# Gram products of a gated delta rule kernel: two runs of one array tile shape each, in place of two shapes in turn

## The chip, the cores and the metric

The kernel runs on one core of a Trainium2 chip. The metric is the device time of one execution in microseconds (us). Before the change three runs gave 435.13, 436.81 and 437.67 us, so the median is 436.81 us. Of one further execution there is a profile, with a trace of every instruction.

## The reference

For 4 x 8 pairs of batch and head there is a state of 48 x 48 numbers. Over 768 steps it is read and corrected, and what it gives goes through two weight matrices with a softplus between them:

```python
k_n = k / (norm(k) + 1e-6)
for t in range(768):
    y[t]  = g[t] * (q[t] @ state)
    state = state + beta[t] * outer(k_n[t], v[t] - state.T @ k_n[t])
x   = y, transposed and reshaped to (3072, 384)
out = softplus(x @ w_in) @ w_out          # w_in 384 x 2048, w_out 2048 x 384
```

## The kernel before

The 768 steps are cut into six rounds of 128 (`cc` in the code), and a round into two chunks of 64 steps (`cl`). Inside a chunk the recurrence is solved in closed form, so that it becomes small matrix products; from chunk to chunk only the state is handed on. The 32 pairs of batch and head are held as p (two groups), i (four pairs of heads), m (which head of the pair) and r (which half of the batches).

A round runs through these stages, and the names are those of the rows further down:

- k, q, v and g are loaded by SP (L299), four transfers for each tensor and round. k is squared on ACT (`ksq`, L380), summed on DVE (L387), brought to a norm (on POOL, L424, from the second round on), and scaled to `kn` (L446); q is cast to `qn` (L467).
- TensorE transposes `kn` and `qn` (L489) and ACT copies the result to `kqt` (L512): features on the partitions, 64 columns of queries and then 64 of keys. Feature rows of m = 0 lie on partitions 0 to 47, those of m = 1 on 64 to 111.
- The Gram products follow (function `gram`), four times in a round, 24 times in all: for each i, r and m a product of the 64 keys with all 128 columns (L531), and a product of the last 32 keys with the 64 keys (L535), which puts two blocks of the key products a second time into other partitions. That is 32 matmuls, each with a weight load of its own. L531 uses a 64 x 64 tile of the array (48 rows by 64 columns are filled), L535 a 64 x 32 tile (48 by 32 filled). Here they are called a gram.
- ACT copies the key products, negated, to `kk` (L553), DVE masks the query products to `mt` (L572). Both read the PSUM buffers that the gram wrote; five buffers of this kind (`p_d`) serve all small products.
- When the four grams of a round are read out, DVE transposes `kk` to `ln` (L595), and a triangular solve of 15 steps follows, on DVE in the first round and on POOL in the others (L617, then L628 and L635). DVE and ACT bring its result back (`tn` L661 and L671, `t` L683 and L691), and small matmuls finish the inverse (L710, L745, L755, L796, L799).
- The state chain goes chunk by chunk through L843, L886, L899, L925, L954, L981, L997 and L1020; the output of a chunk comes from L843 and L1038, is multiplied with g (L1071) and transposed (L1088, L1098).
- The two large products, with w_in (L1122, softplus on ACT in L1143) and w_out (L1160, copied out in L1182 and stored in L1191), fill the rest of TensorE's time. L1122 has 512 moving columns in the four middle rounds, 256 in the first and the last; L1160 has 384.

The order in which each engine gets its instructions is fixed when the program is built. `Plan.run` goes through items with an engine, a cost, dependencies and a priority, and always places the item that can start first. The gram is one item of cost 0.4 and 32 matmuls; what stands inside the item is the planner's only as a number of matmuls. Grams have the priority of an early stage of their round, so those of a round stand among the large products of the rounds before it. Engines take their instructions in order, so an instruction that waits holds up all behind it on its engine.

Of the kernel before, what the change touches and what calls it, by code (L numbers as in the profile page):

```python
# [41 lines left out]
class Plan:  # L42
# [6 lines left out]
    def add(self, eng, cost, fn, deps=(), bufs=(), prio=0, tail=0.1, order=(), mm=0, dma=0):  # L49
        it = Item()  # L50
        it.eng, it.cost, it.fn = eng, cost, fn
        it.deps = [d for d in deps if d is not None]
        it.bufs, it.prio, it.tail, it.end = list(bufs), prio, tail, None
        it.n = len(self.items)
        it.order = [d for d in order if d is not None]
        it.mm, it.dma = mm, dma
        for b in it.bufs:
            b.users += 1
        self.items.append(it)
        return it  # L60
# [94 lines left out]
def kernel(  # L155
# [11 lines left out]
    nc = tc.nc  # L167
    B, H, S, D = q.shape
    P = 128
    C = 64  # L170
    HC = 32
    NSS = S // 128
    NP = H // 2
# [101 lines left out]
    def f16ps(ap):  # L275
        return ap.bitcast(F16)

    HALF = [slice(0, 64), slice(64, 128)]
    FEAT = [slice(0, D), slice(64, 64 + D)]
    QUAD = [slice(32 * i, 32 * i + 32) for i in range(4)]  # L280
# [81 lines left out]
    for cc in range(NSS):  # L362
# [117 lines left out]
        for cl in cls:  # L480
            for p in range(2):
                tp, kq = Buf(p_d), Buf(r_kqt)
                kqt[cl, p] = kq

                def trs(a=kn[cl], b=qn[cl], p=p, tp=tp):
                    o = f16ps(tp.ap).rearrange("p (i r j t) -> p i r j t", r=2, j=2, t=C)
                    for j, x in ((1, a), (0, b)):
                        for i in range(NP):
                            nc.tensor.transpose(  # L489
                                o[:, i, :, j],  # L490
                                x.ap[:, p, 2 * i : 2 * i + 2].rearrange(
                                    "p h d -> p (h d)"
                                ),
                                ident,
                            )

                t1 = add(
                    "PE",
                    0.5,
                    trs,  # L500
                    deps=[kn_it[cl], qn_it[cl]],
                    bufs=[kn[cl], qn[cl], tp, kq],
                    prio=pl + 6,
                    tail=0.2,
                    mm=8,
                )

                kqt_it[cl, p] = [
                    add(
                        "ACT",  # L510
                        1.02,
                        lambda tp=tp, kq=kq: nc.scalar.copy(  # L512
                            kq.ap.rearrange("p n c -> p (n c)"), f16ps(tp.ap)
                        ),
                        deps=[t1],
                        bufs=[tp, kq],
                        prio=pl + 6,
                    )
                ]
                gp = [Buf(p_d), Buf(p_d)]  # L520
                mt[cl, p] = [Buf(r_mt), Buf(r_mt)]

                def gram(kq=kq, gp=gp):


                    for i in range(NP):
                        for r in range(2):
                            for m in range(2):
                                x = kq.ap[FEAT[m], 2 * i + r]
                                o = gp[m].ap.rearrange("p (i c) -> p i c", i=NP)  # L530
                                nc.tensor.matmul(o[HALF[r], i], x[:, C:], x)  # L531
                                o = gp[m].ap.rearrange(
                                    "p (i x c) -> p i x c", i=NP, c=HC
                                )
                                nc.tensor.matmul(  # L535
                                    o[QUAD[2 * r + 1], i, 0:3:2], x[:, C + HC :], x[:, C:]
                                )

                t2 = add(
                    "PE",  # L540
                    0.4,
                    gram,
                    deps=kqt_it[cl, p],
                    bufs=gp + [kq, kk] + mt[cl, p],
                    prio=pl + 6,
                    tail=0.2,
                    mm=32,
                )
                mt_it[cl, p] = []
                for m in range(2):  # L550

                    def kkc(g=gp[m], kk=kk, u0=16 * cl + 8 * p + m):
                        nc.scalar.activation(  # L553
                            kk.ap[:, :, u0 : u0 + 7 : 2].rearrange("p x i t -> p i x t"),
                            g.ap.rearrange("p (i x t) -> p i x t", i=NP, x=4)[:, :, 0:3:2],
                            AF.Copy,
                            scale=-1.0,
                        )

                    kk_it[cl].append(  # L560
                        add(
                            "ACT",
                            0.4,
                            kkc,
                            deps=[t2],
                            bufs=[gp[m], kk],
                            prio=pl + 6,
                        )
                    )

                    def mask_m(g=gp[m], o=mt[cl, p][m]):
                        nc.vector.tensor_tensor(  # L572
                            o.ap,
                            g.ap.rearrange("p (i t) -> p i t", i=NP)[:, :, :C],
                            mask[:, None, :].broadcast_to([P, NP, C]),
                            ALU.mult,
                        )

                    mt_it[cl, p].append(
                        add(  # L580
                            "DVE",
                            0.42,
                            mask_m,
                            deps=[t2],
                            bufs=[gp[m], mt[cl, p][m]],
                            prio=pl + 8,
                        )
                    )
# [114 lines left out]
        for cl in cls:  # L703
            us = range(16 * cl, 16 * cl + 16)
# [20 lines left out]
        for gr in groups:  # L725
            us = slice(16 * gr[0], 16 * gr[-1] + 16)
# [47 lines left out]
        for gr in groups:  # L774
            us = slice(16 * gr[0], 16 * gr[-1] + 16)
# [334 lines left out]
        for job in jobs:  # L1110
# [40 lines left out]
            for gi in [2 * cl + p for cl in job for p in range(2)]:  # L1151
                cl, p = gi // 2, gi % 2
# [73 lines left out]
```

## Time and profile before

| what | value |
|---|---|
| median of three runs | 436.81 us |
| profiled execution | 435.81 us, span of the core's instructions 433.9 us |
| TensorE matmuls busy | 382.2 us (88% of the span), 6384 matmuls |
| DVE, ACT, POOL busy | 139.2, 159.4, 108.5 us |
| mean granted TensorE clock | 0.756 of full speed |
| matmuls of the gram | L531 109.5 us and L535 84.5 us busy, 384 each; their spans overlap one another |
| large products | L1122 85.5 us, L1160 80.5 us busy, 384 each |

A row of the timeline gives start, length, engine, line, operation and shapes, and in brackets how long the engine was idle before it and what ended that. A matmul's end is modelled, so lengths of neighbours overlap: what a matmul costs in a stream is the distance from its start to the next one's start. The granted clock stands as a share of full speed, where 1.00 is 2.4 GHz and 0.50 is 1.2 GHz.

### The profile page before, as it was taken

Reading aid. Unit: us, or ns where it says so; the run is one execution under the profiler, and the core shown is the slowest. Engines: PE = TensorE matmul, PEld = TensorE weight load, DVE = VectorE, ACT = ScalarE, POOL = GpSimd, SP = SyncE. Lnnn points to the kernel's source line nnn. Section 1 sums busy time; section 2 is a strip of 40 time slices with the busy share of each in tenths; the row PEclk is TensorE's granted clock in tenths of the full one; section 3 lists DMA queues with packets and bytes.
Section 4 is the critical chain, followed back from the end, with each engine's and each line's share of the span. In section 5 each row is a group of like instructions: output and inputs, shape, how many; then the busy total and the mean of one; then the engine's idle time right before and its main releaser. Section 6 shows DMA issues by size and latency. Waiting matters only on the chain.

```text
span 433.9 us, 13899 instructions
## 1 busy us (share of the span) xinstructions
PE 382.2 (88%) x6384; PEld 235.1 (54%) x6384; DVE 139.2 (32%) x278; ACT 159.4 (37%) x272; POOL 108.5 (25%) x202
## 2 busy tenths in 40 slices
PE   0699599468899999999999589999999999999895
PEld 0555355355676655455466466546555555656572
DVE  2421950535523131420426133264311054232101
ACT  3331221536572320233354324345141553564250
POOL 7210600385040000740097002228200055000000
PEclk9955555558888855668699555679867979999999
DMA  9999993008910963200011916007100000200202
GB/s 128 170 156 194 174 185 56 2 5 132 156 22 11 149 108 39 54 2 0 2 39 41 147 34 117 2 2 112 38 19 23 3 2 22 57 5 20 56 18 56
DMA packets 106458, 27.73 MB, mean 64 GB/s; under 512 B 100768, under 2 KB 106016, under 8 KB 106400
## 3 DMA queue, kind: packets, MB, share of 16 engines
q1 hardware_dynamic: 103680, 23.60, 35.9%
q0 software_dynamic: 2720, 3.24, 4.4%
q8 instruction: 50, 0.82, 0.9%
q14 instruction: 8, 0.07, 0.1%
HBM read 25.26 MB, written 4.72 MB: 69 GB/s over the span
## 4 chain that ended last, share of the span: by engine, by line
PE 81%; issue 7%; ACT 4%; DVE 3%; SPq 2%; DMA 1%; POOL 1%; ACTq 0%; POOLq 0%; DVEq 0%
PE h L1122 18%; PE d L531 17%; PE o L1160 16%; PE d L535 12%; PE d L489 3%; SPq L299 2%; PE d L843 2%; PE d L1038 2%; PE d L899 2%; PE d L954 2%; PE d L755 1%; PE d L1088 1%; PE d L997 1%; PE d L799 1%; DMA kf<-in_k_dram 1%
## 5 line engine op out<-in xcount | busy, mean ns | idle before, releaser
L531 PE MATMUL d<-kqt 48*64 48x128 f16 x384 | 109.5, 285 | 1.5 <-ACT kqt L512 1.3
L1122 PE MATMUL h<-xt,w_in 128*128 128x512 f16 (+1 forms) x384 | 85.5, 369 | 0.0
L535 PE MATMUL d<-kqt 48*32 48x64 f16 x384 | 84.5, 220 | 0.0
L1160 PE MATMUL o<-w_out,ga 128*128 128x384 f16 x384 | 80.5, 355 | 2.8 <-DVE osb L1182 2.6
L1143 ACT ACTIVATE ga<-h 128x512 f16<-128x512 f32 x96 | 57.1, 598 | 59.4 <-PE h L1122 57.5
L553 ACT ACTIVATE kk<-d 128x256 f16<-128x256 f32 x48 | 18.1, 383 | 126.3 <-PE d L535 100.7
L572 DVE TENSOR_TENSOR mt<-d,mask 128x256 f16<-128x256 f32 x48 | 19.3, 422 | 122.7 <-ACT kk L553 93.1
L531 PEld LDWEIGHTS <-kqt 48*64 48x64 f16 x384 | 44.6, 116 | 25.8 <-issue 2.2
L535 PEld LDWEIGHTS <-kqt 48*32 48x32 f16 x384 | 36.0, 94 | 38.6 <-issue 0.3
L1160 PEld LDWEIGHTS <-ga 128*128 128x128 f16 x384 | 38.6, 105 | 30.8 <-issue 11.3
L1122 PEld LDWEIGHTS <-w_in 128*128 128x128 f16 x384 | 37.6, 106 | 26.1 <-issue 10.9
L424 POOL TENSOR_TENSOR ss<-ss,half_c 128x32 f32<-128x32 f32 (+1 forms) x6 | 27.8, 4631 | 86.1 <-DVE ss L387 86.1
L1182 DVE COPY osb<-o 128x384 f32<-128x384 f32 x24 | 13.3, 555 | 62.1 <-PE o L1160 62.1
L617 POOL TENSOR_TENSOR nn<-ln,beta_l 128x256 f32<-128x256 f16 x10 | 6.0, 617 | 104.6 <-DVE ln L595 104.6
L1071 DVE TENSOR_TENSOR yg<-d,gf 128x384 f16<-128x384 f32 x24 | 13.2, 553 | 54.5 <-PE d L1038 54.3
L635 POOL TENSOR_TENSOR tt<-tt,tmp 128x30 f32<-128x30 f32 (+7 forms) x75 | 28.9, 386 | 5.9
L628 POOL TENSOR_TENSOR tmp<-nn,tt 128x30 f32<-128x30 f32 (+7 forms) x75 | 27.9, 372 | 5.9
L512 ACT COPY kqt<-d 128x1024 f16<-128x1024 f16 x24 | 23.7, 1011 | 14.9 <-PE d L489 14.9
L489 PE MATMUL d<-ident,kn 128*128 128x128 f16 x96 | 13.2, 282 | 12.5 <-DVE kn L446 12.2
L489 PE MATMUL d<-ident,qn 128*128 128x128 f16 x96 | 13.2, 281 | 5.9 <-POOL qn L467 4.6
L925 ACT CAST u<-d 128x384 f16<-128x384 f32 x24 | 11.1, 485 | 16.1 <-PE d L899 16.1
L489 PEld LDWEIGHTS <-kn 128*128 128x128 f16 x96 | 8.9, 129 | 14.8 <-DVE kn L446 12.2
(71 smaller groups left out, 340.1 us busy)
## 6 DMA issues: line engine op xcount, KB each, us to landing
kf<-in_k_dram SPq DMA_DIRECT2D x24, 192.0 KB, 5.5
qf<-in_q_dram SPq DMA_DIRECT2D x24, 192.0 KB, 5.6
vf<-in_v_dram SPq DMA_DIRECT2D x24, 192.0 KB, 4.4
gf<-in_g_dram SPq DMA_DIRECT2D x24, 192.0 KB, 5.4
out_dram<-osb SPq DMA_DIRECT2D x48, 96.0 KB, 2.2
w_in<-in_moe_w_in_dram POOLq DMA_DIRECT2D x1, 1536.0 KB, 11.4
w_out<-in_moe_w_out_dram POOLq DMA_DIRECT2D x1, 1536.0 KB, 15.8
beta_l<-in_beta_dram POOLq DMA_DIRECT2D x8, 12.0 KB, 4.5
```

The source lines that it names most:

```text
L424: lambda ss=ss, r=r: nc.gpsimd.tensor_tensor(ss.ap[:, r], ss.ap[:, r], half_c[:, r], ALU.pow),
L489: nc.tensor.transpose(o[:, i, :, j], x.ap[:, p, 2 * i : 2 * i + 2].rearrange("p h d -> p (h d)"), ident,)
L512: lambda tp=tp, kq=kq: nc.scalar.copy(kq.ap.rearrange("p n c -> p (n c)"), f16ps(tp.ap)),
L531: nc.tensor.matmul(o[HALF[r], i], x[:, C:], x)
L535: nc.tensor.matmul(o[QUAD[2 * r + 1], i, 0:3:2], x[:, C + HC :], x[:, C:])
L553: nc.scalar.activation(kk.ap[:, :, u0 : u0 + 7 : 2].rearrange("p x i t -> p i x t"), g.ap.rearrange("p (i x t) -> p i x t", i=NP, x=4)[:, ...
L572: nc.vector.tensor_tensor(o.ap, g.ap.rearrange("p (i t) -> p i t", i=NP)[:, :, :C], mask[:, None, :].broadcast_to([P, NP, C]), ALU.mult,)
L628: eng.tensor_tensor(t, nn.ap[:, :, j + 1 :, j : j + 1].broadcast_to([P, 2, n, w]), tt.ap[:, :, j : j + 1, 16 : 16 + w].broadcast_to([P, 2, ...
L635: eng.tensor_tensor(rows, rows, t, ALU.add)
L1122: nc.tensor.matmul(hp.ap[:, n * b : n * b + n], w_in[:, j, f * P : (f + 1) * P], xt.ap[:, j, t0 : t0 + n], start=(j == 0), stop=(j == 2),)
L1143: lambda hp=hp, o=gb: nc.scalar.activation(o.ap, hp.ap, AF.Softplus),
L1160: nc.tensor.matmul(op.ap[:, :DM], b.ap[:, c + c0 : c + c0 + 128], w_out[:, f, :], start=(f == 0), stop=(f == NF - 1),)
```

## The change

Inside a gram the 16 matmuls of L531 now come first, in the order of i, r and m, and the 16 of L535 after them in the same order. Operands, targets, the number of matmuls and weight loads, and the item that the planner sees are the same.

```diff
-                    for i in range(NP):
-                        for r in range(2):
-                            for m in range(2):
-                                x = kq.ap[FEAT[m], 2 * i + r]
-                                o = gp[m].ap.rearrange("p (i c) -> p i c", i=NP)
-                                nc.tensor.matmul(o[HALF[r], i], x[:, C:], x)
-                                o = gp[m].ap.rearrange(
-                                    "p (i x c) -> p i x c", i=NP, c=HC
-                                )
-                                nc.tensor.matmul(
-                                    o[QUAD[2 * r + 1], i, 0:3:2], x[:, C + HC :], x[:, C:]
-                                )
+                    us = [(i, r, m) for i in range(NP) for r in range(2) for m in range(2)]
+                    for i, r, m in us:
+                        x = kq.ap[FEAT[m], 2 * i + r]
+                        o = gp[m].ap.rearrange("p (i c) -> p i c", i=NP)
+                        nc.tensor.matmul(o[HALF[r], i], x[:, C:], x)
+                    for i, r, m in us:
+                        x = kq.ap[FEAT[m], 2 * i + r]
+                        o = gp[m].ap.rearrange("p (i x c) -> p i x c", i=NP, c=HC)
+                        nc.tensor.matmul(
+                            o[QUAD[2 * r + 1], i, 0:3:2], x[:, C + HC :], x[:, C:]
+                        )
```

On TensorE, at the start of a gram of the third round that follows an output product (L1038), the order before the change is this; `kqt` is weights and moving data at once, and the last column is the moving shape.

```order
L1038 MATMUL d<-u_2639,mt 64x48
L531 LDWEIGHTS kqt
L531 MATMUL d<-kqt 64x128
L535 LDWEIGHTS kqt
L535 MATMUL d<-kqt 32x2x32
L531 LDWEIGHTS kqt
L531 MATMUL d<-kqt 64x128
L535 LDWEIGHTS kqt
L535 MATMUL d<-kqt 32x2x32
```

At the same place after the change TensorE has the following; a pair of L531 stands where a pair of L535 stood.

```order
L1038 MATMUL d<-u_2639,mt 64x48
L531 LDWEIGHTS kqt
L531 MATMUL d<-kqt 64x128
L531 LDWEIGHTS kqt
L531 MATMUL d<-kqt 64x128
```

In the middle of the same gram, where the shape now changes once, TensorE's order after the change reads as follows.

```order
L531 LDWEIGHTS kqt
L531 MATMUL d<-kqt 64x128
L535 LDWEIGHTS kqt
L535 MATMUL d<-kqt 32x2x32
L535 LDWEIGHTS kqt
L535 MATMUL d<-kqt 32x2x32
```

Around the grams nothing moves: what stands before and behind each of them on TensorE is the same, and so are all rows of DVE, ACT, POOL and SP.

## Rows read from the trace of the kernel before

**Rows 1.** The page, busy time of TensorE: us, share of the span, instructions.
```profile
PE 382.2 (88%) x6384; PEld 235.1 (54%) x6384; DVE 139.2 (32%) x278; ACT 159.4 (37%) x272; POOL 108.5 (25%) x202
```

**Rows 2.** The page, chain that ended last, shares of the span by line.
```profile
PE h L1122 18%; PE d L531 17%; PE o L1160 16%; PE d L535 12%; PE d L489 3%; SPq L299 2%; PE d L843 2%; PE d L1038 2%; PE d L899 2%; PE d L954 2%; PE d L755 1%; PE d L1088 1%; PE d L997 1%; PE d L799 1%; DMA kf<-in_k_dram 1%
```

**Rows 3.** Stretches: length; busy PE, PEld, DVE, ACT, POOL; granted clock; DMA, GB/s.
```profile
98.00:133.00 35.00, 30.25 (x873) 23.49 (x871) 15.33 (x29) 22.10 (x36) 11.20 (x4) 0.83 0.61 100
133.00:219.00 86.00, 85.58 (x663) 46.15 (x663) 23.76 (x44) 23.49 (x44) 15.81 (x33) 0.68 0.29 45
219.00:237.00 18.00, 17.01 (x654) 11.80 (x657) 7.29 (x15) 7.22 (x12) 15.58 (x35) 1.00 0.17 41
237.00:348.00 111.00, 103.65 (x1937) 63.16 (x1923) 31.06 (x61) 42.17 (x74) 20.58 (x38) 0.71 0.30 50
348.00:434.00 86.00, 77.78 (x1413) 48.12 (x1409) 23.20 (x45) 35.80 (x62) 12.04 (x32) 0.98 0.13 30
```

**Rows 4.** Timeline of PE at the end of a gram of the third round.
```profile
152.95 0.31 PE L531 MATMUL d<-kqt 48*64 48x128 f16 x1
153.19 0.23 PE L535 MATMUL d<-kqt 48*32 48x64 f16 x1
153.35 1.46 PE L1160 MATMUL o<-w_out,ga 128*128 128x384 f16 x4
```

**Rows 5.** The page, groups of the gram: busy us, mean ns, idle before.
```profile
L531 PE MATMUL d<-kqt 48*64 48x128 f16 x384 | 109.5, 285 | 1.5 <-ACT kqt L512 1.3
...
L535 PE MATMUL d<-kqt 48*32 48x64 f16 x384 | 84.5, 220 | 0.0
```

**Rows 6.** Timeline of PE, small products of one tile shape in a stream.
```profile
99.54 0.44 PE L843 MATMUL d<-s,kqt 48*64 48x48 f16 x32
99.91 0.37 PE L954 MATMUL d<-u,z 32*32 32x48 f16 x16
...
296.92 0.21 PE L997 MATMUL d<-u,kn 64*64 64x48 f16 x2
296.95 0.19 PE L1038 MATMUL d<-u,mt 64*64 64x48 f16 x2
```

**Rows 7.** Timeline of PE, ACT and DVE, first gram and what reads it.
```profile
18.05 0.24 PE L531 MATMUL d<-kqt 48*64 48x128 f16 x1 [0.84 <-ACT kqt L512]
...
23.71 0.71 ACT L553 ACTIVATE kk<-d 128x256 f16<-128x256 f32 x2 [4.80 <-DVE mt L572]
```

**Rows 8.** Timeline of DVE, first two rounds: masks and the end of the solve.
```profile
42.61 0.82 DVE L572 TENSOR_TENSOR mt<-d,mask 128x256 f16<-128x256 f32 x2 [5.31 <-PE d L535]
...
58.77 0.19 DVE L635 TENSOR_TENSOR tt<-tt,tmp 128x30 f32<-128x30 f32 x1
...
62.77 0.82 DVE L572 TENSOR_TENSOR mt<-d,mask 128x256 f16<-128x256 f32 x2 [3.15 <-ACT kk L553]
...
77.71 0.82 DVE L572 TENSOR_TENSOR mt<-d,mask 128x256 f16<-128x256 f32 x2 [5.58 <-ACT kk L553]
```

**Rows 9.** Loads: SP's timeline, second round's q; the page's issue of w_in.
```profile
23.83 6.10 SPq L299 DMA_DIRECT2D qf<-in_q_dram  x4
...
w_in<-in_moe_w_in_dram POOLq DMA_DIRECT2D x1, 1536.0 KB, 11.4
```

**Rows 10.** Timelines around the solve of the fourth round.
```profile
215.93 5.44 POOL L424 TENSOR_TENSOR ss<-ss,half_c 128x32 f32<-128x32 f32 x1 [25.37 <-DVE ss L387]
...
237.06 1.04 DVE L661 STREAM_TRANSPOSE tn<-tt 128x512 f32<-128x512 f32 x1
...
244.89 1.34 PE L710 MATMUL d<-tn,kk 16*32 16x16 f16 x128 [1.62 <-ACT tn L671]
...
249.71 0.25 PE L843 MATMUL d<-s,kqt 48*64 48x48 f16 x3 [2.93 <-issue]
```

**Rows 11.** L1160 alone by stretch: length, PE and PEld busy, clock, DMA.
```profile
133.00:219.00 86.00, 17.89 (x60) 6.71 (x60) 0.68 0.29 45
...
237.00:348.00 111.00, 14.37 (x64) 7.13 (x64) 0.71 0.30 50
348.00:434.00 86.00, 34.80 (x192) 18.51 (x192) 0.98 0.13 30
```

## The prediction

> **What bounds the kernel now.** I read the page's busy shares first. TensorE's matmuls are busy 88% of the span, and ACT, the next engine, 37% [rows 1]. The chain that ended last says whether that engine also sets the end: 63% of the span lies on four of its lines, 29% of it on the two lines of the gram (17% L531, 12% L535), which is 125.8 us of 433.9 [rows 2]. Then the stretches: from 133 to 219 us PE is busy 85.6 of 86 us and from 237 to 348 us 103.7 of 111 us, and these two hold 16 of the 24 grams. The three other stretches shown hold none (but for the first three records of the ninth gram, at 132.7 us), and there the granted clock is 0.83, 1.00 and 0.98 against 0.68 and 0.71 [rows 3]. So where grams stand PE is full, and its clock falls.
>
> Why a gram is dear shows in the timeline. From one L531 to the L535 behind it 0.24 us pass, and from that to the next instruction 0.16 us: 0.40 us for a pair [rows 4]. At 1.2 GHz 128 columns take 0.107 us and 64 take 0.053 us, so some 0.13 and 0.11 us of each are not columns. Over all grams the page's means give the same by another way: neighbours overlap by 0.07 us in the rows, so a pair costs 285 + 220 - 140 = 365 ns, and 384 pairs 140.2 us [rows 4, 5].
>
> Two other readings must be set aside. Weights and moving data from `kqt` are not slow as such: 32 matmuls of L843, with weights from the same tile and the same 48 x 64 shape, start within 0.37 us, 11.6 ns each. Nor is it changing lines: L997 and L1038 alternate two by two and take 0.03 us for two; both use 64 x 64 tiles [rows 6]. What L531 and L535 do not share is the tile's shape, 64 against 32 columns. I take that for the cause.
>
> **The price of a gram after the change.** The same 32 matmuls and weight loads remain, with two changes of shape (in the middle and at an end) for 32. No row shows 128 moving columns in a 64 x 64 tile in a stream. Below, 32 matmuls at L843's pace are 0.37 us [rows 6]. Above, if the four tiles shared nothing and the clock were 1.2 GHz, 16 x 107 + 16 x 53 ns are 2.56 us. I stay near the L843 row, whose tiles and turns (m and r) are the same: a mean of 96 columns in place of 48 makes 0.74 us, and two changes at 0.13 us make **1.0 us**, against 5.8 on average now. The bounds move 24 grams by -15 and +37 us, less in the early stage, where PE is not alone on the chain.
>
> [...]
>
> **The sum, stage by stage.** It starts from the profiled execution's 435.8 us (span 433.9 and 1.9 around it).
>
> First two rounds, 18 to 98 us. The first gram starts at 18.05 when ACT's copy is there [rows 7], and does not move. Now the masks of round one end at 43.4 [rows 8]. After, a gram must still wait until the previous one's buffers are read: 1.0 us, a mask of 0.41 (half of a row of two), a `kk` copy of 0.36 and some 0.2 of hand-overs, 2.0 us a turn [rows 7, 8]. So the fourth gram ends at 18.05 + 3 x 2.0 + 1.0 = 25.1 and the masks at 25.9, 17.5 us sooner. Behind this DVE's solve of the first round, now ending at 58.96 beside grams of the second round [rows 8], becomes the thing to wait for: it moves by 17.5 us to 41.4 and no more. From there to the last mask 19.6 us pass now (58.96 to 78.53). Their last two grams cost 12.8, and shrink to 2; so do some 0.7 us of the second gram's wait. The last mask then comes near 49.5, 29 us sooner. What can be late is the data: q of the second round is issued until 29.9, and a w_in issued earlier, behind an earlier `kn` on POOL, may push it by as much as its own 11.4 us [rows 9]; of that up to 6 us would show. I take 2: **27 us** saved (23 to 29).
>
> The sixteen later grams. Of the first eight, four stand between 18.05 and about 42.6 us [rows 7, 8] and four run at 16 x 0.40 us, 50.2 us together, so the others take 140.2 - 50.2 = 90.0. Before them PE is all but full [rows 3], so they come off the end as they are: 90.0 - 16 x 1.0 = **74.0 us**. Nothing moves on any engine's order, and no wait is added in the code.
>
> What is late next, when PE runs sooner to its waits. The fourth round's solve is the tightest: POOL's root at 215.93, its solve, and DVE's `tn` at 237.06 to 238.10; about a us later L710 could start, at 239.2. It starts at 244.89, after a wait of 1.62 on an ACT copy that itself waits behind a gram [rows 10]. Without 4.6 us of gram L710 would be due at 238.7: the wait is 0.5 us, so the chain on POOL just holds. The other solves have more work on PE ahead of them. Instruction supply is the second: at 249.71 PE stood 2.93 us for nothing but issue [rows 10], and now 64 instructions pass in 1 us in place of 6. Bounds: nothing, or eight more such stops, 23 us. I take two, **+5 us**.
>
> The clock. L1160 costs 17.89 / 60 = 298 ns in the first gram stretch, 225 in the second, and 181 in the last 86 us without grams [rows 11]. At 181 ns its 60 + 64 matmuls would save 7.0 + 2.8 us, and L1122, with 18% of the chain where L1160 has 16% [rows 2], about as much: 20 us if the clock stays at 2.4 GHz, none if it does not. Grams of 1 us in place of 6 leave the large products closer together, as in the stretch with 0.98, but PE may also wait more. I take a little over half, **-12 us**.
>
> Sum: 435.8 - 27 - 74.0 + 5 - 12 = 327.8 us. The median shown is 1.0 above the profiled execution, so **329 us**.
>
> **The rivals.**
> 1. Other work takes PE's place at once (chance 0.17). For it: the second round's q is still being issued at 29.9 us [rows 9], and every `tn` hangs on DVE, POOL and ACT in order [rows 10]. Against it: ACT is at 37% and POOL at 25% [rows 1]. Loads late by 12 in the early stage leave 15 there, waits take 28 of the 74, and the clock gives nothing: 435.8 - 15 - 46 + 1 = 376; its lighter half lies from 354 up.
> 2. All goes better (0.03): a gram at 0.5 us saves 12 more, the clock its whole 20 us, no stop is added: 329 - 12 - 8 - 5 = 304.
> 3. The change does not do what it says (0.03): a run of one shape pays the same 0.40 us per two, because what is slow is 128 columns or a bank written by two row halves. Then 437. Against it stands L843.
> 4. Slower (0.02): short grams starve PE, and the clock then stays at 1.2 GHz where the large products are. By their columns at 1.2 GHz (192 matmuls of 512, 192 of 256, 384 of 384) they are 246 us; now they hold 34% of the span on the chain, some 148 [rows 2]. So +98 and 25 of waits against -101: 458. It decides once the large products lose over 76 us beside those waits. Against it: the stretches without grams have 0.83 to 1.00 [rows 3]. [...]
>
> **How the numbers follow.** The forecast has 0.75, with its own range of 306 to 354: the bounds of the gram's price, 0 to 23 us of stops and 0 to 20 us of clock around 329. Rival 1 adds a little from below its own time, and some 5 in 100 of the forecast's own case fall outside, so about 8 in 10 lie in it. Within 0.5%, which is what this kernel's measurement can tell from no change, lies rival 3 (0.02 of it); above lie rival 4 and the rest. Faster 0.95, same 0.02, slower 0.03.
>
> **What would show it.** In the profile after: L531 in runs of 16 and a gram's first start to the next instruction near 1 us (right from 0.4 to 2.6; wrong at 5); the masks of round one over by 26 to 30 us; the solve of the first round ending near 42; the first L1122 near 70 in place of 98; the granted clock over 0.8 between the first L1122 and the last gram; PE's busy time near 255 us. The forecast is wrong if the grams shrink and the idle time of PE grows by more than 30 us over the 52 it has now: then the rows of waits say which of POOL, DVE or the loads took over.

## The result and the profile after

The changed kernel takes 322.22 us (319.77 to 323.56, four runs) against 437.24 us (435.13 to 440.27, four runs) of the kernel before: a ratio of 0.7359, 95% interval 0.7295 to 0.7423. It takes 26% less time; 329 us were predicted, with a range of 306 to 354. Runs over 1.5% above the fastest of their kernel are left out of ratios and comparisons between kernels; of the changed kernel that leaves six in two series, 318.56 to 323.56 us, median 321.87. The profiled execution took 322.74 us, span 320.9, which is 113.0 us less than the span before.

First the page: busy us, share of the span and instructions of each engine; the chain that ended last, by line; then groups of instructions with busy us, mean ns, and idle time before them.

```profile
PE 242.5 (76%) x6384; PEld 160.9 (50%) x6384; DVE 134.9 (42%) x278; ACT 157.4 (49%) x272; POOL 109.3 (34%) x202
...
PE o L1160 19%; PE h L1122 19%; SPq L299 8%; DMA kf<-in_k_dram 4%; DMA qf<-in_q_dram 4%; PE d L489 3%; PE d L843 3%; PE d L1038 2%; PE d L954 2%; POOL tt L635 2%; PE d L899 2%; PE d L755 2%; POOL tmp L628 2%; PE d L799 2%; PE d L710 2%
...
L531 PE MATMUL d<-kqt 48*64 48x128 f16 x384 | 13.4, 258 | 4.3 <-ACT kqt L512 2.9
```

The same 6384 matmuls are there, and PE is busy 139.7 us less [rows 1]. L531 was 17% and L535 12% of the chain [rows 2]; neither is among its lines now. L531's busy time went from 109.5 to 13.4 us, while the mean of one record only went from 285 to 258 ns [rows 5]. So a single matmul's record is hardly shorter: they lie over one another now. What has come onto the chain are loads: 16% (SP's issue, k and q), where SP's issue and k had 3% [rows 2].

Two grams in the timeline of PE (start, us, instruction, how many in a row):

```profile
18.15 0.64 PE L531 MATMUL d<-kqt 48*64 48x128 f16 x16 [0.91 <-ACT kqt L512]
18.72 0.40 PE L535 MATMUL d<-kqt 48*32 48x64 f16 x16
19.06 0.31 PE L531 MATMUL d<-kqt 48*64 48x128 f16 x1
...
110.11 0.42 PE L531 MATMUL d<-kqt 48*64 48x128 f16 x16
110.46 0.30 PE L535 MATMUL d<-kqt 48*32 48x64 f16 x16
110.69 0.50 PE L1160 MATMUL o<-w_out,ga 128*128 128x384 f16 x2
```

Start to start, the first gram takes 0.57 + 0.34 = 0.91 us, the one at 110 us 0.35 + 0.23 = 0.58 us. The first is at the lower level of the clock: its single L531 record is 0.31 us long, as in [rows 4]. Before, a gram took 16 pairs of 0.40 us, 6.4 us, at that level [rows 4], and less at the higher one. From the kernel before, a gram at the higher level (its first record, then the product behind it), and two stretches inside the gram of [rows 4], with columns as in [rows 3]:

```profile
196.20 0.24 PE L531 MATMUL d<-kqt 48*64 48x128 f16 x1
...
201.01 0.66 PE L1160 MATMUL o<-w_out,ga 128*128 128x384 f16 x3
...
148.00:150.00 2.00, 2.00 (x19) 1.27 (x14) 0.56 (x1) 0.00 (x0) 0.00 (x0) 1.00 0.77 130
151.00:153.00 2.00, 2.00 (x12) 1.09 (x11) 0.00 (x0) 0.00 (x0) 0.00 (x0) 0.50 1.00 178
```

That gram takes 4.8 us, so at like clocks the change is from 6.4 to 0.91 us and from 4.8 to 0.58 us. In the gram of [rows 4] the clock falls from one level to the other while PE is busy all the time. In the kernel before the levels show as paces: at a granted 0.50 twenty L489 products of 128 columns take 2.13 us (120.56 to 122.69), 107 ns each, 1.2 columns per ns; at 1.00 twelve L1122 products of 256 columns take 1.31 us (397.49 to 398.80), 109 ns each, and sixteen L1160 products of 384 take 2.60 us (405.62 to 408.22), 162.5 ns each, so 128 columns more take 53 ns, 2.4 per ns. It is as these paces that the rows show the levels called 1.2 and 2.4 GHz.

Stretches of the later part (length; busy PE, PEld, DVE, ACT, POOL; granted clock; DMA, GB/s), cut where [rows 3] were cut by events, the third round's first gram and the last gram's end:

```profile
74.00:110.00 36.00, 30.95 (x894) 24.09 (x879) 15.40 (x29) 21.90 (x35) 6.19 (x3) 0.86 0.58 97
110.00:164.00 54.00, 50.29 (x1292) 30.51 (x1290) 29.87 (x59) 29.89 (x55) 32.01 (x67) 0.97 0.45 84
164.00:237.00 73.00, 60.72 (x1950) 39.60 (x1948) 31.14 (x61) 41.98 (x74) 20.63 (x38) 0.81 0.46 76
237.00:321.00 84.00, 75.65 (x1397) 47.13 (x1397) 23.08 (x45) 35.82 (x63) 12.07 (x32) 1.00 0.13 31
```

From the third round's first gram to the end 301 us passed before, 211 now. The two gram stretches have granted clocks of 0.97 and 0.81 in place of 0.68 and 0.71. PE's idle time in this part is 3.7 + 12.3 + 8.4 = 24.4 us, against 17.0 before (length less busy in the last four rows of [rows 3]): 7.4 us more. The stretch from 110 to 164 us holds the work of two of [rows 3], 133 to 219 and 219 to 237 us. The same cuts for L1160 alone (PE and PEld busy), with a stretch of the kernel before that [rows 11] leave out:

```profile
110.00:164.00 54.00, 22.66 (x108) 9.78 (x108) 0.97 0.45 84
164.00:237.00 73.00, 11.39 (x64) 6.06 (x64) 0.81 0.46 76
237.00:321.00 84.00, 34.81 (x192) 18.50 (x192) 1.00 0.13 31
...
219.00:237.00 18.00, 9.00 (x48) 4.12 (x48) 1.00 0.17 41
```

A product of L1160 takes 210, 178 and 181 ns. The same 108, 64 and 192 products took 249, 225 and 181 ns before: the 108 are 60 at 298 ns [rows 11] and 48 at 187 ns, together 26.89 us. L1122 from the third round's first gram to the end, before and after:

```profile
132.67:433.90 301.23, 70.96 (x289) 27.91 (x288) 0.80 0.24 42
110.11:320.90 210.79, 62.60 (x289) 25.93 (x288) 0.93 0.33 60
```

The early stage, in the timelines of DVE, POOL, SP, ACT and PE (the bracket is the idle time before, and what ended it); the last row is the kernel before:

```profile
24.55 0.76 DVE L572 TENSOR_TENSOR mt<-d,mask 128x256 f16<-128x256 f32 x2 [0.25 <-PE d L535]
...
37.47 0.19 DVE L635 TENSOR_TENSOR tt<-tt,tmp 128x30 f32<-128x30 f32 x1
42.89 0.75 DVE L572 TENSOR_TENSOR mt<-d,mask 128x256 f16<-128x256 f32 x2 [5.23 <-ACT kk L553]
...
47.76 0.75 DVE L572 TENSOR_TENSOR mt<-d,mask 128x256 f16<-128x256 f32 x2 [0.16 <-ACT kk L553]
...
38.88 0.82 POOL L467 CAST qn<-qf 128x768 f16<-128x768 f32 x1 [9.70 <-DMA qf<-in_q_dram]
...
25.46 11.36 SPq L299 DMA_DIRECT2D qf<-in_q_dram  x4
...
57.28 0.84 ACT L380 ACTIVATE ksq<-kf 128x768 f32<-128x768 f32 x1 [4.94 <-DMA kf<-in_k_dram]
58.03 1.93 ACT L691 CAST td<-t 128x1024 f16<-128x1024 f32 x1
...
60.01 0.40 PE L745 MATMUL d<-td,ident 32*32 32x256 f16 x4 [6.43 <-ACT td L691]
...
74.23 1.01 PE L1122 MATMUL h<-xt,w_in 128*128 128x256 f16 x4
...
84.98 0.40 PE L745 MATMUL d<-td,ident 32*32 32x256 f16 x4 [1.38 <-ACT td L691]
```

The masks of round one are over at 25.3 us and those of round two at 48.5, in place of 43.4 and 78.5 [rows 8]: 30 us sooner. The first product with w_in, at 97.77 before, starts at 74.23, only 23.5 us sooner. The 6.5 us between are longer waits, some 5 of them one wait: PE waits 6.43 us for `td` where it waited 1.38. The load of k for the third round lands late; ACT waits 4.94 us for it with `ksq`; `td` is queued behind `ksq` on ACT, and PE waits for `td`. The wait on k thus reaches PE through an instruction that has nothing to do with k. The second round's q is late too: its issue takes 11.36 us where it took 6.10 [rows 9], and POOL waits 9.70 us for it with `qn`, which the second round's grams need. DVE's solve of the first round is over at 37.66 us, 5.2 us before the first mask of round two.

### The profile page after: what moved, and what is told of

It reads as the page before. It is cut to its first block, busy times and chain, and to the rows that moved or that the text cites. A ratio compares the mean times of both kernels' runs of the same rounds, so it can differ in the third digit from the quotient of the medians.

```text
span 320.9 us, 13899 instructions
## 1 busy us (share of the span) xinstructions
PE 242.5 (76%) x6384; PEld 160.9 (50%) x6384; DVE 134.9 (42%) x278; ACT 157.4 (49%) x272; POOL 109.3 (34%) x202
## 4 chain that ended last, share of the span: by engine, by line
PE 62%; DMA 8%; issue 8%; SPq 8%; ACT 5%; POOL 5%; DVE 4%; ACTq 0%; POOLq 0%
PE o L1160 19%; PE h L1122 19%; SPq L299 8%; DMA kf<-in_k_dram 4%; DMA qf<-in_q_dram 4%; PE d L489 3%; PE d L843 3%; PE d L1038 2%; PE d L954 2%; POOL tt L635 2%; PE d L899 2%; PE d L755 2%; POOL tmp L628 2%; PE d L799 2%; PE d L710 2%
## 5 line engine op out<-in xcount | busy, mean ns | idle before, releaser
L1122 PE MATMUL h<-xt,w_in 128*128 128x512 f16 (+1 forms) x384 | 77.0, 341 | 1.0 <-ACT ga L1143 0.9
L1160 PE MATMUL o<-w_out,ga 128*128 128x384 f16 x384 | 73.6, 333 | 2.8 <-DVE osb L1182 2.6
L1160 PEld LDWEIGHTS <-ga 128*128 128x128 f16 x384 | 36.5, 99 | 27.3 <-issue 5.8
L1122 PEld LDWEIGHTS <-w_in 128*128 128x128 f16 x384 | 35.4, 101 | 22.1 <-issue 3.4
L489 PE MATMUL d<-ident,qn 128*128 128x128 f16 x96 | 12.4, 269 | 15.9 <-POOL qn L467 14.7
L572 DVE TENSOR_TENSOR mt<-d,mask 128x256 f16<-128x256 f32 x48 | 18.1, 415 | 14.6 <-ACT kk L553 13.2
L553 ACT ACTIVATE kk<-d 128x256 f16<-128x256 f32 x48 | 16.3, 382 | 12.9 <-PE d L535 9.5
L489 PE MATMUL d<-ident,kn 128*128 128x128 f16 x96 | 12.4, 269 | 12.5 <-DVE kn L446 12.2
L387 DVE TENSOR_REDUCE ss<-ksq 128x16 f32<-128x768 f32 x12 | 11.3, 945 | 19.3 <-ACT ksq L380 19.3
L380 ACT ACTIVATE ksq<-kf 128x768 f32<-128x768 f32 x12 | 10.2, 848 | 16.1 <-DMA kf<-in_k_dram 14.6
L489 PEld LDWEIGHTS <-qn 128*128 128x128 f16 x96 | 8.8, 124 | 16.5 <-POOL qn L467 15.0
L531 PE MATMUL d<-kqt 48*64 48x128 f16 x384 | 13.4, 258 | 4.3 <-ACT kqt L512 2.9
L489 PEld LDWEIGHTS <-kn 128*128 128x128 f16 x96 | 8.3, 122 | 16.1 <-DVE kn L446 12.2
```

Of the source, the lines that this page charges most:

```text
L489: nc.tensor.transpose(o[:, i, :, j], x.ap[:, p, 2 * i : 2 * i + 2].rearrange("p h d -> p (h d)"), ident,)
L553: nc.scalar.activation(kk.ap[:, :, u0 : u0 + 7 : 2].rearrange("p x i t -> p i x t"), g.ap.rearrange("p (i x t) -> p i x t", i=NP, x=4)[:, ...
L572: nc.vector.tensor_tensor(o.ap, g.ap.rearrange("p (i t) -> p i t", i=NP)[:, :, :C], mask[:, None, :].broadcast_to([P, NP, C]), ALU.mult,)
L1122: nc.tensor.matmul(hp.ap[:, n * b : n * b + n], w_in[:, j, f * P : (f + 1) * P], xt.ap[:, j, t0 : t0 + n], start=(j == 0), stop=(j == 2),)
L1160: nc.tensor.matmul(op.ap[:, :DM], b.ap[:, c + c0 : c + c0 + 128], w_out[:, f, :], start=(f == 0), stop=(f == NF - 1),)
```

## The experiments

Theory: a matmul in a tile of another shape than the one before it pays some 0.13 us or more, and that makes the gram dear. Rivals: the two products of a unit disturb each other, because they share key rows and a bank of the result; it is the turn of tile positions that matters; the gain of one stage is given back in another. The diffs are against the changed kernel. There, `one` stands for the body of its first loop (L531) and `two` for that of its second (L535), each for one unit of `us`.

**Shapes still alternate, but no two neighbours belong together.**

```
-    for i, r, m in us: ... (one)
-    for i, r, m in us: ... (two)
+    for n in range(17):
+        if n < 16:
+            one(*us[n])
+        if n > 0:
+            two(*us[n - 1])
```

> The two shapes still take turns (29 changes of shape in a gram of 32 matmuls), but each product of the last 32 keys now follows the big product of the next unit, so neighbours share neither PSUM bank, nor target, nor row half, nor weights. Theory (a change of tile shape costs about 0.13 us at 2.4 GHz, from (0.30 - 0.036) / 2, and 0.17 us at 1.2 GHz, from (0.40 - 0.057) / 2): a gram stays at 4.3 to 5.8 us and the kernel at 415 to 437 us. Rival (the second product waits because it writes over what the first has just written, in the same bank and rows): a gram falls to 0.6 to 1.5 us and the kernel to 320 to 340 us.

Measured: 434.41 us (433.42 and 435.40), beside 432.78 us of the kernel before. The timeline of PE in its first gram:

```profile
18.27 0.23 PE L537 MATMUL d<-kqt 48*32 48x64 f16 x1
18.43 0.31 PE L532 MATMUL d<-kqt 48*64 48x128 f16 x1
18.67 0.23 PE L537 MATMUL d<-kqt 48*32 48x64 f16 x1
```

A pair is 0.16 + 0.24 = 0.40 us, to the hundredth what [rows 4] show, with another unit's product as neighbour. What the expectation says of the neighbours holds for one step of the two. By the order of `us`, the step from L532 to L537 joins products that share neither a row half nor a result buffer, but the step from L537 to the next L532 joins two of one row half and one result buffer. Before it was the other way round, and the two steps take 0.24 and 0.16 us in both kernels. So sharing rows or a buffer moves neither step, and that rival falls.

**Turns as before, but one shape.** The product of 64 keys is cut into two of 32, so that all 48 matmuls of a gram use 32-column tiles:

```
     def one(i, r, m):
...
-        nc.tensor.matmul(o[HALF[r], i], x[:, C:], x)
+        nc.tensor.matmul(o[QUAD[2 * r], i], x[:, C : C + HC], x)
+        nc.tensor.matmul(o[QUAD[2 * r + 1], i], x[:, C + HC :], x)
...
+    for u in us:
+        one(*u)
+        two(*u)
```

> The order of before, unit by unit in turn, but the big product is cut into two of 32 keys, so all 48 matmuls of a gram use 64 x 32 tiles; the output is the same. Theory (shape): no change of shape inside a gram, 48 matmuls at some 20 to 30 ns, 0.7 to 1.4 us for a gram, the kernel at 320 to 335 us in spite of 16 more matmuls and weight loads. Rival (taking turns between products of 128 and 64 columns, or writing twice to one place, is what costs): a gram stays above 4.8 us, the kernel above 430 us.

Measured: 325.54 us (325.51 and 325.58). The timeline of PE, the first record of the third round's first gram and the product behind that gram:

```profile
110.56 0.23 PE L532 MATMUL d<-kqt 48*32 48x128 f16 x1
...
111.13 0.82 PE L1167 MATMUL o<-w_out,ga 128*128 128x384 f16 x4
```

The gram takes 0.57 us with 48 matmuls in turns, as long as the 32 in runs at the higher level (0.58 us). Taking turns between products of 128 and 64 columns costs nothing seen here once both have one shape: nearly the whole gain is there without any runs. With the run before, this shows the cause: the change of tile shape.

**Runs of four in place of sixteen** (in place of the two loops), so eight changes of shape per gram in place of two:

```
+    for n in range(0, 16, 4):
+        for u in us[n : n + 4]:
+            one(*u)
+        for u in us[n : n + 4]:
+            two(*u)
```

> Runs of four instead of sixteen: four of the one shape, then four of the other, four times in a gram, 7 changes of shape instead of 1. Theory (a fixed price for each change): 6 more changes at 0.13 us (2.4 GHz) or 0.17 us (1.2 GHz), a gram at 1.36 or 1.94 us, the kernel at 335 to 342 us. Rival (a run must be long to get its weight loads ahead, so that a short run loses most of the gain): a gram at 2.5 us or more, the kernel at 360 us or more.

Measured: 327.48 and 333.04 us (the profile is of the second), lower than expected. The timeline of PE, in the first gram and some 3 us later:

```profile
18.39 0.25 PE L532 MATMUL d<-kqt 48*64 48x128 f16 x4 [0.93 <-ACT kqt L512]
18.57 0.21 PE L537 MATMUL d<-kqt 48*32 48x64 f16 x4
18.71 0.25 PE L532 MATMUL d<-kqt 48*64 48x128 f16 x4
...
21.17 0.32 PE L532 MATMUL d<-kqt 48*64 48x128 f16 x4
21.42 0.24 PE L537 MATMUL d<-kqt 48*32 48x64 f16 x4
21.59 0.32 PE L532 MATMUL d<-kqt 48*64 48x128 f16 x4
```

Four and four take 0.32 us, later 0.42: a gram is 1.28 or 1.68 us. Against 0.58 and 0.91 of the changed kernel, six more changes make 0.70 and 0.77 us, 0.12 and 0.13 us each. A gram of before has 32 changes, 30 more than the changed kernel's: (4.8 - 0.58) / 30 = 0.14 us each at the higher level and (6.4 - 0.91) / 30 = 0.18 us at the lower. So a change costs 0.12 to 0.18 us, and the price is not fixed: it is less in runs of four than in turns. The time rose by less than 24 times the 0.7 us. In the early stage nearly all of the rise is hidden: the third round's first gram starts at 110.69 us, where it starts at 110.11 in the changed kernel.

**Runs of sixteen, but the same tile four times in a row**, in place of a new tile at every matmul:

```
-    us = [(i, r, m) for i in range(NP) for r in range(2) for m in range(2)]
+    us = [(i, r, m) for m in range(2) for r in range(2) for i in range(NP)]
```

> Two runs of 16 as after the change, but with row half and column half outermost, so four matmuls in a row use the same tile of the array before the next tile's turn comes. My price of a gram rested on four tiles sharing the time. [...] If weight loads overlap and only the columns add up: 1.3 us at 2.4 GHz, the kernel at 333 to 343 us. If the turn of tiles does not matter: 0.57 and 0.91 us as after the change, the kernel at 320 to 324 us.

Measured: 320.50 and 328.57 us, the changed kernel's time within what two runs tell. The timeline of PE, again in the first gram and a little later:

```profile
18.52 0.45 PE L532 MATMUL d<-kqt 48*64 48x128 f16 x16 [1.28 <-ACT kqt L512]
18.90 0.33 PE L537 MATMUL d<-kqt 48*32 48x64 f16 x16
...
21.46 0.68 PE L532 MATMUL d<-kqt 48*64 48x128 f16 x16 [0.56 <-ACT kqt L512]
22.07 0.43 PE L537 MATMUL d<-kqt 48*32 48x64 f16 x16
```

Sixteen products take 0.38 us here and 0.35 us with turning tiles; at the lower level 0.61 and 0.57. So the turn of positions, on which the prediction leaned with the L843 row, is worth a few hundredths of a microsecond, and beside the price of the shape that is small.

**Runs in the first two rounds only, and in the last four only.** A first attempt at both read a variable of the building loop after the loop had ended, so that all grams took the same order. The one came out as the kernel before again, the other as the changed kernel again:

> Runs of one shape in the grams of the first two rounds only, turns as before in the other 16. My sum: what the early stage saves, 23.5 us by the two traces (first w_in product at 97.8 before, 74.2 after), should come off alone, 436.8 - 23.5 = 413 us (409 to 417), and between the first w_in product and the last gram the granted clock should stay near 0.7. Rival (an early gain is given back behind, because the later rounds are held by the loads or the solves and not by PE): 425 us or more.

Measured: 439.21 us beside 438.66 of before (ratio 1.001, 0.996 to 1.006; one of its ten runs took 1208.09 us, for a reason that is not known), a repeat of before that tells nothing of the stages.

> Turns as before in the first two rounds, runs in the other 16 grams. By the two traces the stretch from the first gram of the third round to the last gram takes 215.1 us before and 126.5 after, 88.7 us saved: 348 us (344 to 352), and the granted clock in it rises from 0.7 to about 0.9, since it is the slow grams beside the large products that bring it down there. Rival (the clock rises because the whole kernel is denser, early stage included): the clock of that stretch stays below 0.8 and the kernel is at 356 us or more.

Measured: 322.93 us (318.56 to 327.14; ratio 0.7325, 0.7248 to 0.7402), a repeat of the changed kernel. Its runs serve below. The second attempt ties the round to each gram:

```
-    def gram(kq=kq, gp=gp):
+    def gram(kq=kq, gp=gp, cc=cc):
...
+        if cc < 2:      # the other kernel: cc >= 2
+            for u in us:
+                one(*u)
+            for u in us:
+                two(*u)
+        else:
+            for u in us:
+                one(*u)
+                two(*u)
```

> The run with this idea before it took its condition from the loop's last round, so that all its grams took turns as before; here runs of one shape stand in the first two rounds and turns in the other 16 grams. Sum by the two traces: the early stage's 23.5 us come off alone, 411 to 418 us against 437 to 440 before, and the granted clock between the first w_in product and the last gram stays near 0.7. Rival (an early gain is given back behind): 425 us or more.

Measured: 416.32 us (414.38 to 419.46), ratio 0.9483 (0.9408 to 0.9557): 23.4 us under the 439.74 beside it.

> As above, its twin: turns as before in the first two rounds, runs in the other 16 grams (the run before it had runs of one shape everywhere and stands for the changed kernel). By the two traces 88.7 us come off between the first gram of the third round and the last gram: 344 to 352 us, with the clock of that stretch near 0.9. Rival (the clock there rises only if the early stage is dense too): 356 us or more and a clock below 0.8 in it.

Measured: 347.57 us (345.80 to 348.62), ratio 0.7907 (0.7852 to 0.7962): 92.2 us under. The third round's stretch in the first kernel, where its grams take turns, and then in the second (columns as in [rows 3]):

```profile
110.00:194.00 84.00, 84.00 (x653) 45.43 (x651) 21.38 (x41) 20.65 (x40) 12.74 (x32) 0.64 0.29 46
```

```profile
133.00:187.00 54.00, 50.30 (x1336) 31.18 (x1338) 31.22 (x61) 30.69 (x56) 31.64 (x65) 1.00 0.45 86
```

Each part alone gives 23.4 + 92.2 = 115.6 us, both together 115.0 (the two medians of the result): the stages add up, and nothing gained in one is given back in another. And with grams in turns this stretch has a granted clock of 0.64, with grams in runs 1.00. Over the longer stretches that the expectations name it is 0.74 (first w_in product to last gram) and 0.88 (third round's first gram to last gram), near the 0.7 and 0.9 expected.

**Another order of loads.** The theory on the 6.5 us lost in the early stage was that the loads of q (second round) and k (third round) come too late. So they are put ahead of w_in, of g and of the second round's v; w_out is put behind that v:

```
-                deps=[tiles["v", 0, 1][1]],      # w_in
+                deps=[tiles["k", 2, 1][1]],
...
-                deps=[tiles["q", 1, 1][1]],      # w_out
+                deps=[tiles["v", 1, 1][1]],
...
-    weights()
-    load("g", g, r_g, 0)
     load("q", q, r_q, 1)
-    weights2()
-    load("v", v, r_v, 1)
     load("k", k, r_k, 2)
+    load("g", g, r_g, 0)
+    weights()
+    load("v", v, r_v, 1)
+    weights2()
     load("g", g, r_g, 1)
```

> The kernel after the change with other loads first: q of the second round and k of the third ahead of g of the first, w_in issued after them, w_out after v of the second. In the trace after the change POOL stood 9.7 us for q and ACT 4.9 us for k. Theory (in the early stage the loads have taken the place of PE): both waits go, DVE's solve of the first round sets the time, the first w_in product moves from 74.2 to 65 to 69 us, and the kernel is 4 to 9 us faster than 322, 313 to 318 us. Rival (w_in or v, now later, are waited for instead, or the gain is lost behind): 320 us or more.

Measured: 317.18 us (315.42 to 319.69; ratio 0.7273, 0.7219 to 0.7327), 4.7 under the changed kernel's median of six, with ranges that overlap. But the first product with w_in stands at 74.53, where 65 to 69 was expected. The timelines of DVE, then PE:

```profile
67.76 0.56 DVE L467 CAST qn<-qf 128x768 f16<-128x768 f32 x1 [13.98 <-DMA qf<-in_q_dram]
...
72.23 0.19 PE L843 MATMUL d<-s,kqt 48*64 48x48 f16 x1 [5.01 <-DVE s L1018]
...
74.53 0.80 PE L1122 MATMUL h<-xt,w_in 128*128 128x256 f16 x3
```

The two waits that were aimed at went (the one on q is 2.89 us, that on k is gone). A third took their place, in the same form: DVE waits 13.98 us for the third round's q, `s` is queued behind it, and PE waits for `s`. PE also stands 4.46 us for its own issue, at 56.62. The time was right and its place wrong, so the agreement is luck: what gain there is came after this point (the third round's first gram stands at 106.98, 3.1 us sooner), and why there was not followed up.

**That q ahead as well**, before the second round's v and w_out (here the diff is against the kernel just shown):

```
-                deps=[tiles["v", 1, 1][1]],      # w_out
+                deps=[tiles["q", 2, 1][1]],
...
+    load("q", q, r_q, 2)
     load("v", v, r_v, 1)
     weights2()
     load("g", g, r_g, 1)
     for cc in range(2, NSS):
-        load("q", q, r_q, cc)
+        if cc > 2:
+            load("q", q, r_q, cc)
```

> As the run with other loads first, and q of the third round ahead of v of the second, w_out after it. In that run the first w_in product stood at 74.5 us as in the changed kernel, because DVE waited 14 us for q of the third round ahead of the state copy, and PE 5.0 us for that. Theory (loads set the early stage, each wait removed shows the next): that wait goes, the first w_in product comes at 67 to 71 us, and the kernel at 309 to 315 us. Rival (the supply of instructions and the order on DVE take the time instead, or it is lost behind): 316 us or more.

Measured: 315.94 us (314.51 to 316.75), ratio 0.7183 (0.7126 to 0.7241). Its timelines of DVE, then PE:

```profile
58.56 0.80 DVE L469 CAST qn<-qf 128x768 f16<-128x768 f32 x1 [8.01 <-DMA qf<-in_q_dram]
...
56.86 0.41 PE L757 MATMUL d<-td,xs 32*16 32x16 f16 x37 [4.49 <-issue]
...
66.51 0.43 PE L956 MATMUL d<-u,z 32*32 32x48 f16 x13 [2.55 <-issue]
71.64 1.46 PE L1124 MATMUL h<-xt,w_in 128*128 128x256 f16 x6
```

The wait on q is 8.01 in place of 13.98 us and the product with w_in 2.9 us earlier; PE loses 4.49 and 2.55 us there to its own issue, as it lost 4.46 and 1.73 with the load order before. The kernel just misses the 309 to 315 us expected, and the product the 67 to 71. All its runs lie below the eight of the changed kernel in its two series (318.56 to 327.14): it is the fastest found, some 6 us (2%) under it. Whether it beats the load order before it, with 315.42 to 319.69, is not settled.

## Why the prediction was right, and where its sizes were off

- **The cause** (a change of tile shape) is shown, by the alternating shapes without shared rows and by the one shape in turns. The runs show that a new tile of one shape at each matmul costs no more than the same one again (0.35 us for sixteen products, against 0.38) and that a new shape costs 0.12 to 0.18 us, here between tiles of 64 and of 32 columns.
- **The gram's price, 1.0 us**, was too high: 0.91 at the lower level, 0.58 at the higher. The step took L843's pace, scaled to 96 columns a matmul, as the mean. The matmuls overlap more than that: at the higher level, which is the level of the L843 row, products of 128 columns start 22 ns apart, where that scaling gives 31. With m outermost, where eight matmuls in a row use the same row half, sixteen take 0.38 us.
- **The early stage, 27 us**, came to 23.5, inside its bounds of 23 to 29. The masks of round one were followed well (25.3 for 25.9). Those of round two agree by luck (48.5 for 49.5): the sum had them wait for DVE's solve, moved to 41.4 "and no more". But the solve was over at 37.66, and what the grams of round two waited for was q. The term that was mis-sized is that of late loads, 2 us taken and 6 the bound: 6.5 us went between the last mask and the first product with w_in. That q's issue would get longer was right (6.10 to 11.36 us), but this wait took the solve's place ahead of the masks; the wait that reached PE behind them was on the third round's k, which the sum did not name, through ACT's queue.
- **The sixteen later grams, 74.0 us**, came to some 80: 90.0 less 16 times about 0.6.
- **The clock, 12 us.** From the first gram of the third round to the end 301.2 - 210.8 = 90.4 us were saved. With 80.4 of grams and 7.4 of new idle time this leaves 17.4 us by which PE's other work became shorter. The large products have 15.6 of it: L1160 (26.89 + 14.37) - (22.66 + 11.39) = 7.2 and L1122 70.96 - 62.60 = 8.4. The direction is that of [rows 11], and kernels that differ in the late grams alone show it as well: 0.68 before against 1.00 with runs in the late grams only, and 0.97 after against 0.64 with runs in the early ones only.
- **New waits, 5 us**, came to 7.4 of idle time. The stops for issue were there: 3.32, 2.30 and 2.38 us are the longest in that part. The timeline of PE shows the longest, and the wait of the fourth round's L710, predicted at 0.5 us:

```profile
167.09 1.19 PE L710 MATMUL d<-tn,kk 16*32 16x16 f16 x128 [1.69 <-ACT tn L671]
...
172.15 0.25 PE L843 MATMUL d<-s,kqt 48*64 48x48 f16 x3 [3.32 <-issue]
```

- **Sum.** Between the first w_in product and the third round's first gram 1.0 us more passed than before. 23.54 - 0.98 + 90.44 = 113.0 us, where 27 + 74 - 5 + 12 = 108 was the net of the terms. The later grams gave some 6 us more and the clock 5 more; the early stage gave 4.4 less and the waits took 2.4 more. So 329 stands as near to 322 as it does because misses of both signs cancel in part.
- **The rivals.** The first, other work in PE's place, took place in part: PE's idle time grew by 26.7 us, under the 30 that were named. Of this 7.4 are late; the other 19.3 are early, where eight grams gave up about 43 us (50.2 to some 7) and the time only 23.5. It did not decide, as 16 of 24 grams stand where PE is full. Of the second, the gram (0.58 for 0.5) and most of the clock came, the absence of stops did not. That the change does nothing, and that short grams starve PE and slow its clock, both fall.
- **What was to be seen.** PE's busy time came to 242.5 us for 255, the first L1122 to 74.2 for "near 70", the end of the first solve to 37.7 for "near 42", the granted clock to 0.97 and 0.81 in the two gram stretches for "over 0.8".

## What to carry to other kernels

Where small matmuls of two tile shapes alternate, look at the timeline from start to start: a pair far longer than its columns, with single records that overlap little, may be the price of the shape (here 0.40 us for 192 columns, which at the 1.2 columns per ns of that level are 0.16 us). Here it went by sorting the instructions into runs of one shape or by giving both one shape. What such a saving is worth is read stage by stage: here it was had in full where the engine had no idle time, and about half of it where it waits for a chain. Then look at what each in-order queue holds behind a load: in the changed kernel and with the first new load order, the wait that reached TensorE (6.43 and 5.01 us) was for a cast queued behind an instruction that waited for other data.

## What the runs showed of the hardware

- Sixteen products of 128 columns in one run take 0.35 us with four tiles in turn and 0.38 with each tile four times in a row. One after another, at the pace of L1160's 384 columns in 181 ns, they would take an estimated 0.97 us. That the order of tiles matters so little was not expected.
- The granted clock of the first part of a span must be held against the lengths of matmuls. In the changed kernel's profile the rows before 74 us have 1.00, while a single L531 takes 0.31 us at 19.06, as in [rows 4] at a granted 0.50. The kernel with runs in the first rounds only, which does the same there, shows 0.52 from 18 to 74 us. The mean clock of a whole run differs likewise, 0.935 in the run of 322.74 us and 0.848 in that of 321.69, so such means aren't compared here.
- Stops of TensorE for issue alone, of over 1 us, stand in stretches of many small matmuls: nine in the changed kernel, of 1.1 to 3.3 us, where there were five before, of 1.2 to 2.9 us; the longest seen, 4.49 us, is in the kernel with the last order of loads. What they wait for was not tried.
